# The last 64 rows of v copied in DRAM once per batch, one load of 96 rows per unit, and an order planned with longer issue times

## The chip, the cores and the metric

The kernel runs on one core of a Trainium2 chip. The metric is the device time of one execution in microseconds (us), the median of three runs. The engines are TensorE (PE, with its weight loads PEld), VectorE (DVE), ScalarE (ACT), GpSimd (POOL) and SyncE (SP); SP issues nearly all DMAs, into one hardware queue that 16 DMA engines serve. L12 is line 12 of the kernel before.

## The reference

An attention of two parts over 8 batches, 8 heads, 576 positions and 64 columns a head, then a feed-forward block over the 4,608 tokens. All numbers are fp32.

```python
q_d, k_d, v_d = (x.reshape(B, H, S // 4, 4, D).mean(axis=3) for x in (q, k, v))
out_up = np.repeat(sm_attn(q_d, k_d, v_d), 4, axis=2)      # attention of the means of four rows
mask = np.abs(pos[:, None] - pos[None, :]) < 4              # and a band of 7 positions
scores = np.where(mask, scale * q @ k.T, -1e9)
out_local = softmax(scores) @ v
x = (out_up + out_local).transpose(0, 2, 1, 3).reshape(4608, 512)
h = x @ w_in                                                # 512 x 2048
out = (h * np.clip(h + 3, 0, 6) / 6) @ w_out                # 2048 x 512
```

The change touches `v_d`, the sums of four rows of v. Of 144 such sums a head, 128 fill the 128 partitions, and 16 are left over: those of the last 64 rows of v.

## The kernel before

**Work.** Attention is cut into 32 units: a batch b and a pair of heads hp (four pairs). The feed-forward block is cut into nine chunks of 512 tokens; a chunk has 16 blocks f of 128 of the 2,048 columns. For each f, `gemm1` (L1053, matmuls at L1059) forms h, ACT and DVE apply the gate (L1065, L1069), `hi` and `lo` (L1071, L1075, both through L121, L119 or L1077) split it into a rounded part and a rest, and `gemm2` (L1104, L1109) adds its share of the output. An fp32 product is three matmuls of such parts. The last two chunks are computed together by sums and differences of blocks (L1141 on). A chunk needs the attention of its tokens, so attention and feed-forward work are interleaved.

**A unit.** q and k come in with four DMAs each (`ldt`, L373), and DVE turns them (`turn`, L379) and sums them by fours (`pool4`, L411 on DVE). v comes in by windows (`ldv`, L433), and for the sums of four rows by `ld4`: `ld4(0)` loads 128 rows of 2 KB, four rows of v each (L439), and `ld4(1)` the last 64 rows of v. In units of which the probabilities of both heads are multiplied together (26 of the 32) the 16 rows of 2 KB are wanted four times, on partitions 0, 16, 64 and 80, so `ld4(1)` is four DMAs of 16 rows (L444). `sum4` (L446) sums them by fours, multiplies with a mask by head and clears partitions 32 to 63 and 96 to 127. Units 0 to 5 ("alone") load the 64 rows with one DMA (L441). Probabilities go through DRAM to be turned: the downsampled ones by `pd` (`put_d` L612, `get_d` L620 and L625), the local ones by `pl` (`put` L639, `get` L647). The sum of both parts is written by `add` (L766 on DVE); the parts of x split from that are what `gemm1` reads.

**Bursts.** From unit 8 on PE's attention work stands in bursts (`plan_burst`, L329): the scores of a new unit (L523, L668, L718) and the products with v of the unit two before it (L761).

**Order.** The program is straight-line code, and a list scheduler writes its order: `Plan.emit` (L1798) has a cost for every operation (`COST`, and numbers at the call of `op`), due times from `T0`, `TC`, `TF` and `UNIT_T`, moved for each unit by `SHIFT`, and gives each engine the ready operation that is due first. Where an operation may run on several engines, `PEN` holds what an engine adds to its due time. DMAs are modelled by `Queue` (L1723): the time to issue one (`BEGUN`), to serve it (`PACKET`) and to land (`LAND`), and a ring of eight, since every DMA waits for the semaphore of the DMA eight before it. Each engine executes its list in order, so an instruction that waits holds all behind it on its engine. Dummy matmuls (L1449) stand in front of the first GEMM.

Of the kernel before, what the change touches and what calls it, by code (L numbers as in the profile page):

```python
# [8 lines left out]
F32 = mybir.dt.float32  # L9
# [8 lines left out]
B, H, S, D = 8, 8, 576, 64  # L18
DM, DFF = 512, 2048
P = 128  # L20
# [36 lines left out]
def tile_local_down_attention_moe(ctx, tc, q_all, k_all, v_all, _qk_loc, _v_loc, w_in, w_out, ident_d, _mask_d, out):  # L57
# [179 lines left out]
    def src(t, first, ap):  # L237
        return bass.AP(tensor=t.tensor, offset=t.offset + first * ROW, ap=ap)
# [117 lines left out]
    def plan_unit(b, d, u, row0, k0, kv, PS, masked, early_user, due):  # L356
# [62 lines left out]
        for kind, t in (("q", q_all), ("k", k_all)):  # L419
            hk = kind, un  # L420
            if b < BY_PE:
                a = turned[kind] = [evs["qk".index(kind)], evs[2]]
            else:
                l = op("SP", 2.0, partial(ldt, t, kind), loads if b == 1 else [], take=[("qk", hk)], size=dma(4 * S, 128), nd=4)
                a = turned[kind] = [op("DVE", 0.72, partial(turn, kind), [l], lag=BEHIND[0 if b == 1 else 1])]
            pooled[kind] = early_user(op(
                on("pool4", 1.0), 0, partial(pool4, kind), a, take=[("p4" + k0, hk)]))
# [8 lines left out]
        def ld4(g):  # L436
            st["raw", g] = raw = buf("raw" + k0, ("v", un, g), [P, 4, ROW])
            if g == 0:
                nc.sync.dma_start(raw, src(v_all, row0, [[4 * ROW, P], [1, 4 * ROW]]))  # L439
            elif alone:  # L440
                nc.sync.dma_start(raw[:4 * KR, 0], src(v_all, row0 + 4 * P, [[ROW, 4 * KR], [1, ROW]]))  # L441
            else:
                for first in (0, KR, D, D + KR):
                    nc.sync.dma_start(raw[first:first + KR], src(v_all, row0 + 4 * P, [[4 * ROW, KR], [1, 4 * ROW]]))  # L444

        def sum4(g, eng):  # L446
            if "vd" not in st:
# [35 lines left out]
        if direct:  # L483
            sums = [begun["vr"], op({"POOL": on("sum4", 1.0)["POOL"]}, 0, partial(sum4, 0), [begun["v", d]],
                                    take=[("vd" + k0, un)], free=[("raw4", (0, d))])]
        for g in range(0 if direct else 2):
            rk = "raw" + k0, ("v", un, g)
            l = op("SP", 0.5, partial(ld4, g), take=[rk], size=dma(P, 512) if alone and g else dma((P, 2 * NAR)[g], 2048), nd=1 if alone else 1 + 3 * g)
            if alone and g:
                bk = PS, ("v4", un, g)  # L490
                a = op("PE", 0.34, partial(sum_pe, g), [l], take=[bk], free=[rk], lag=LAGT, rec=2)
                sums.append(op(on("ev", ROW), 0, partial(evict_v, g), [a], take=[("vd" + k0, un)], free=[bk]))
            else:
                sums.append(op(on("sum4", 1 + g), 0, partial(sum4, g), [l], take=[("vd" + k0, un)], free=[rk], lag=BEHIND[3]))

# [546 lines left out]
    def plan_moe(n):  # L1042
# [6 lines left out]
        for f in range(NF):  # L1049
# [42 lines left out]
            last1 = a  # L1092
            gemms.append(a)
            b = op("ACT", 0.04 + size / 1130, relu, [a], take=[("t" + k0, ("t", key))])
            c = op("DVE", 0.07 + size / 960, gate, [b], free=[("h", key)])
            d = op(on("ghi", size), 0, hi, [c], take=[("gh" + k0, ("gh", key))], lock=True)
            st["ready"] = [d, op(on("gl", size), 0, lo, [d], take=[("gl" + k0, ("gl", key))], free=[("t" + k0, ("t", key))],
                                 lock=True)]
# [390 lines left out]
        plan.emit(warm, gemms[0], busy)  # L1489


T0, TC, TF, LAG = 60.12, 81.59, 5.26, 2.0
UNIT_T = (4.0, 20.34, 23.11, 24.0, 25.01, 24.0, 24.0, 21.51)
EARLY = 0.7
SLACK = (3.35, 24.0, 49.24, 41.62, 33.95, 31.63, 36.96, 13.02)
PRE, GATE = 4, 14

AHEAD = 2

FIRST = 6.8, 2.92  # L1500


HK = DM // 2
# [19 lines left out]

EARLY_Z = 14, 28

LAGT = 0.5

BEHIND = [-0.29, 0.65, 0.0, -0.16]

LAGW = 2.16  # L1530

# [1 line left out]
ORDERED = ("raw", "qk", "v", "vd", "P", "Pd", "Pl", "PT", "od", "p4", "st", "a", "o0", "o1", "o2", "o3", "z", "sx", "ue", "uo", "ghb", "glb")  # L1533
HOP, FREE = 0.1, 0.1

BOTH, KEEP = ("h0x", "h1x"), -7.57

MARGIN = 0.43

PAIR0 = 8  # L1540

SHIFT = [
# [4 lines left out]
]  # L1547

STAY = 8.33

IDLE, COLD = (0.22, 0.1, 0.75), 7.2

# [2 lines left out]
PACKET = {64: 38, 128: 11.5, 512: 27.5, 576: 27, 1024: 50, 2048: 88, 4096: 170}  # L1555
BEGUN = {64: 0.41, 128: 0.52, 512: 0.67, 576: 0.65, 1024: 0.36, 2048: 0.45, 4096: 0.47, (512, 640): 0.49, (2048, 36): 0.4, (128, 384): 0.49}
LAND = {64: 1.3, 128: 1.25, 512: 2.0, 576: 1.45, 1024: 1.2, 2048: 1.5, 4096: 1.65, (512, 640): 1.2}
FRESH, TURNED, LANDS, SHORT = (3.2, 18.0, (512, 2048), 1.6), (0.7, 25.0), (2.4, 6.0), 0.16
HOPS = {("ACT", "DVE"): 0.14, ("ACT", "PE"): 0.19, ("ACT", "POOL"): 0.16, ("DVE", "ACT"): 0.13, ("DVE", "PE"): 0.19, ("DVE", "POOL"): 0.2,
        ("PE", "ACT"): 0.2, ("PE", "DVE"): 0.2, ("POOL", "ACT"): 0.075, ("POOL", "DVE"): 0.075, ("POOL", "PE"): 0.1,  # L1560
# [17 lines left out]
    "pull": {"ACT": (0.22, 0.0), "DVE": (0.17, 0.0)},  # L1578
}
PEN = {  # L1580
    "lo": {"DVE": 2.22},
    "low": {"DVE": 8.81},
    "whi": {"DVE": 12.96},
    "ghi": {"DVE": -5.51},
    "pool4": {"POOL": 26.99},
    "ev": {"DVE": 5.81},
    "sum4": {"POOL": -4.99},
    "norm": {"DVE": 68.37},
    "normd": {"DVE": 46.75, "ACT": 23.63},
    "minus": {"DVE": -10.56},  # L1590
    "xhi": {"DVE": 31.2},
    "xlo": {"POOL": -27.96},
    "gl": {"POOL": 5.88},
    "ob": {"DVE": 12.47},
    "pull": {"DVE": 0.92},
}


# [119 lines left out]
def dma(packets, size):  # L1718

    return Load([(packets, size)])  # L1720


class Queue:  # L1723
# [7 lines left out]
    def begin(self, t, size, n):  # L1731
        k = n // len(size.parts)
        for packets, each in [(p / k, e) for p, e in size.parts for _ in range(k)]:
            t = max(t, self.slot()) + BEGUN.get((each, round(packets)), BEGUN[each])
            while self.queued and sum(p for at, p in self.queued if at > t) + packets / 16 > QUEUED:
                left = [at for at, _ in self.queued if at > t]
                if not left:
                    break
                t = min(left)
            self.queued = [x for x in self.queued if x[0] > t]  # L1740
            took = service(packets, each)
            if each in FRESH[2] and FRESH[0] < t < FRESH[1]:
                took *= FRESH[3]
            took = max(took, SHORT) + (TURNED[0] if t > TURNED[1] and self.big != (each == 4096) else 0.0)
            self.big = each == 4096
            self.flow = max(self.flow, t + (LANDS[0] if t < LANDS[1] else LAND[each, round(packets)] if (each, round(packets)) in LAND else LAND[each])) + took
            self.landed.append(self.flow)
            self.queued.append((self.flow, packets / 16))
        return t, self.flow


class Plan:
# [5 lines left out]
    def op(self, eng, cost, fn, after=(), take=(), free=(), size=0, dl=None, lag=0.0, lock=False, rec=0, nd=1, kind=None):  # L1758
        o = Op(len(self.ops), eng, cost, fn, take, size, dl)
        o.kind = kind  # L1760

        o.rec, o.nd = rec, nd
        o.lag, o.lock = lag, {True: ("DVE", "POOL"), False: ("POOL",)}[lock]
        self.ops.append(o)
        for a in after:
            self.dep(o, a)
        for r in free:
            self.free_after(r, [o])
        return o
# [308 lines left out]
```

## Time and profile before

| | us |
|---|---|
| median of three runs (899.37 to 902.68) | 900.11 |
| the profiled execution | 899.97 |
| its span | 898.2 |
| PE busy | 883.5 (98%) |
| DVE busy | 628.1 (70%) |
| ACT busy | 402.4 (45%) |
| POOL busy | 219.4 (24%) |

The granted TensorE clock is 1.00 over the whole span. The chain that ended last is PE for 90%, SP's queue for 3%, DMA for 3%. A chain of waits is followed back from the last instruction to what released it; where it lies on PE, PE has work, and where it leaves PE, something came late. The windows show in which stretch that is.

### The profile page before, as it was taken

The page shows a single profiled execution, that of the slowest core. Times are in us where ns is not written, and L with a number is a line of the kernel's source. Part 1 is how long each engine was busy: PE and PEld are TensorE (multiplying, and loading weights), DVE is VectorE, ACT ScalarE, POOL GpSimd, SP SyncE. Part 2 cuts the span into 40 slices and gives each one's busy share as a digit, 9 for nine tenths or more (in the row PEclk, how much of TensorE's full clock was granted, in tenths as well). Part 3 has the DMA queues.
Part 4 walks back from the last instruction along what each step waited for, and adds up shares of the span by engine and source line. Part 5 has one row for each costly group of instructions (what it writes and reads, how often), then busy time and mean ns, then how long its engine had stood idle before and what let it go on. Part 6 is the DMA issues. An engine that isn't in the chain of part 4 may idle for free.

```text
span 898.2 us, 19662 instructions
## 1 busy us (share of the span) xinstructions
PE 883.5 (98%) x7067; PEld 720.6 (80%) x7067; DVE 628.1 (70%) x1182; ACT 402.4 (45%) x1397; POOL 219.4 (24%) x292
## 2 busy tenths in 40 slices
PE   8999999999999999999999999999999999999998
PEld 6677878887887888888887888888778888888886
DVE  7998988766766467676767666567666899965430
ACT  6787644545474145444544426144443444331100
POOL 4554633232232011211111312103222125301000
PEclk9999999999999999999999999999999999999999
DMA  9999576556566356655367516857657002223011
GB/s 228 204 284 327 128 174 129 114 117 127 99 147 129 67 106 133 130 113 104 78 141 148 115 33 142 244 121 178 147 121 181 2 24 70 87 78 117 17 31 48
DMA packets 325985, 111.95 MB, mean 125 GB/s; under 512 B 258687, under 2 KB 306943, under 8 KB 325887
## 3 DMA queue, kind: packets, MB, share of 16 engines
q1 hardware_dynamic: 325206, 109.92, 52.1%
q8 instruction: 56, 0.92, 0.4%
q10 hardware_dynamic: 680, 0.77, 0.3%
q14 instruction: 43, 0.34, 0.1%
HBM read 79.58 MB, written 31.05 MB: 123 GB/s over the span
## 4 chain that ended last, share of the span: by engine, by line
PE 90%; SPq 3%; DMA 3%; DVE 2%; ACT 1%; issue 1%; ACTq 0%; DVEq 0%
PE o L1109 32%; PE h L1059 32%; PE o L1407 5%; PE o L1292 4%; PE a L1407 2%; PE h L1407 2%; PE a L1292 2%; PE h L1292 2%; PE a L718 2%; PE h L761 1%; PE a L523 1%; DMA arena<-in_k_dram 1%; DMA arena<-in_q_dram 1%; PE h L668 1%; PE a L506 1%
## 5 line engine op out<-in xcount | busy, mean ns | idle before, releaser
L1109 PE MATMUL o<-wp,rounded 128*128 128x512 f32 x1344 | 322.7, 392 | 0.0
L1059 PE MATMUL h<-rounded,wp 128*128 128x512 f32 x1344 | 315.5, 390 | 4.6 <-DVE arena L766 3.3
L1059 PEld LDWEIGHTS h<-rounded,wp 128*128 128x128 f32 x1344 | 251.3, 188 | 59.4 <-issue 6.3
L1109 PEld LDWEIGHTS o<-wp,rounded 128*128 128x128 f32 x1344 | 249.7, 188 | 53.4 <-issue 0.4
L1065 ACT ACTIVATE arena<-h 128x512 f32<-128x512 f32 x112 | 66.5, 594 | 114.8 <-PE h L1059 113.6
L1069 DVE SCALAR_TENSOR_TENSOR arena<-arena,h 128x512 f32<-128x512 f32 x112 | 76.0, 678 | 42.3 <-ACT arena L1065 41.8
L1077 DVE TENSOR_TENSOR rounded<-arena,rounded 128x512 fp32r<-128x512 f32 x80 | 58.0, 725 | 37.1 <-PE o L1109 35.5
L573 ACT ACTIVATE arena<-arena 128x64 f32<-128x64 f32 x240 | 80.1, 336 | 0.4
L1077 POOL TENSOR_TENSOR rounded<-arena,rounded 128x512 fp32r<-128x512 f32 x32 | 43.8, 1370 | 129.5 <-PE o L1109 72.7
L119 ACT CAST rounded<-arena 128x512 fp32r<-128x512 f32 (+6 forms) x61 | 38.8, 640 | 49.5 <-DVE arena L1069 24.3
L121 DVE CAST rounded<-arena 128x512 fp32r<-128x512 f32 (+2 forms) x89 | 40.3, 455 | 28.9 <-PE o L1109 10.5
L379 DVE STREAM_TRANSPOSE arena<-arena 128x576 f32<-128x576 f32 x56 | 43.0, 769 | 24.6 <-DMA arena<-in_k_dram 12.8
L454 POOL TENSOR_TENSOR arena<-arena 96x256 f32<-96x256 f32 (+1 forms) x32 | 24.2, 756 | 138.3 <-DMA arena<-in_v_dram 134.7
L693 ACT ACTIVATE arena<-h 128x144 f32<-128x144 f32 x24 | 7.0, 291 | 96.7 <-PE h L677 96.6
L573 ACT ACTIVATION_READ_ACCUMULATOR arena<-arena 128x1 f32 x240 | 45.2, 188 | 0.0
L1407 PE MATMUL o<-wp,rounded 128*128 128x512 f32 (+1 forms) x204 | 43.8, 376 | 0.0
L1407 PEld LDWEIGHTS o<-wp,rounded 128*128 128x128 f32 x204 | 36.8, 188 | 7.1
L411 DVE TENSOR_REDUCE arena<-arena 128x144 f32<-128x576 f32 x53 | 38.6, 739 | 2.8 <-PE h L523 2.7
L455 POOL TENSOR_TENSOR arena<-arena 96x128 f32<-96x128 f32 (+1 forms) x32 | 15.1, 471 | 81.8 <-PE h L677 80.3
L452 DVE TENSOR_REDUCE arena<-arena 128x128 f32<-128x512 f32 (+1 forms) x22 | 23.7, 1078 | 15.8 <-PE h L668 6.9
L635 DVE STREAM_TRANSPOSE arena<-arena 128x384 f32<-128x384 f32 (+1 forms) x52 | 23.4, 464 | 14.5 <-DMA arena<-pd 14.0
L654 DVE STREAM_TRANSPOSE arena<-arena 128x640 f32<-128x640 f32 x26 | 21.9, 841 | 14.8 <-DMA arena<-pl 14.4
(260 smaller groups left out, 1206.4 us busy)
## 6 DMA issues: line engine op xcount, KB each, us to landing
arena<-in_v_dram SPq DMA_DIRECT2D x58, 160.0 KB
pl<-arena SPq DMA_DIRECT2D x26, 320.0 KB
arena<-pl SPq DMA_DIRECT2D x104, 80.0 KB
rawp<-in_w_in_dram SPq DMA_DIRECT2D x16, 512.0 KB
rawp<-in_w_out_dram SPq DMA_DIRECT2D x16, 512.0 KB
arena<-in_q_dram SPq DMA_DIRECT2D x112, 72.0 KB
arena<-in_k_dram SPq DMA_DIRECT2D x112, 72.0 KB
arena<-in_v_dram SPq DMA_DIRECT2D x28, 256.0 KB
```

The lines of the kernel that those rows point to most:

```text
L119: nc.scalar.copy(out_, in_)
L121: eng.tensor_copy(out_, in_)
L379: nc.vector.transpose(out=qk[kind], in_=qk[kind])
L411: eng.tensor_reduce(out=t, in_=x.rearrange("e (q r) -> e q r", r=4), op=ALU.add, axis=AX.X)
L573: nc.scalar.activation(x[:, j], x[:, j], AF.Exp, bias=m[:, j:j + 1], scale=0.125, accum_out=s[:, j:j + 1])
L1059: nc.tensor.matmul(st["ps"], win[f][:, wt, kk * P:(kk + 1) * P], xs[part][:, kk], start=(kk == 0 and i == 0), stop=(kk == NK - 1 and i == ...
L1065: nc.scalar.activation(st["t"], st["ps"], AF.Relu, bias=3.0)
L1069: nc.vector.scalar_tensor_tensor(out=t, in0=t, scalar=6.0, in1=st["ps"], op0=ALU.min, op1=ALU.mult)
L1077: eng.tensor_tensor(st["gl"], st["t"], st["gh"].bitcast(F32), op=ALU.subtract)
L1109: nc.tensor.matmul(otile[n, m], gt[:, ms], wout[f][:, wt], start=(f == 0 and i == 0), stop=(f == NF - 1 and i == 2),)
L1292: nc.tensor.matmul(ps[which], stationary(w, wt, kb), xs[x, kb][:, part], start=first and kb == 0 and q == 0, stop=last and kb == 1 and q = ...
L1407: nc.tensor.matmul(otile[n, m][:, cs], gt[:, ms], wout[f][:, wt, cs], start=(f == order[0] and i == 0), stop=(f == order[-1] and i == 2 an ...
```

## The change

`ends` is new. Once for each batch from 1 to 7 it copies, from DRAM to DRAM, the last 64 rows of v of all four pairs of heads, six times each: 24 pieces of 32 KB. `ld4(1)` then is one DMA of 96 rows of 2 KB from that copy, in place of the four of 16 rows; the 96 rows are six times the 16, so partitions 0 to 31 and 64 to 95 hold what they held before. The copy of batch b is planned behind a mark, the k load of unit 3 for the copy that follows batch 1 and of unit 1 of the previous batch for the others (the first two have none), and the 96-row load depends on the copy of its batch. That is 78 DMA issues less and 7 more.

The planner's gate costs 0.07 us more (at c), its issue times are 1.06 times and its landings 0.25 us longer behind 130 us (`SLOWER`), and the tables are others: `T0`, `LAG`, `UNIT_T`, `SLACK`, `FIRST`, `LAGT`, `BEHIND`, `KEEP`, `MARGIN`, `SHIFT`, `STAY`, `PEN`. Lines after L425 stand 2 to 13 further down in the changed kernel: L433 is L435, L439 is L441, L444 is L446, L766 is L777, L1059 is L1070.

```diff
@@ plan_unit @@
+                if kind == "k" and hp == (3 if b == 1 else 1):
+                    begun["mark", b] = [l]
...
-                for first in (0, KR, D, D + KR):
-                    nc.sync.dma_start(raw[first:first + KR], src(v_all, row0 + 4 * P, [[4 * ROW, KR], [1, 4 * ROW]]))
+                t = begun["ends", b]
+                nc.sync.dma_start(
+                    raw[:D + 2 * KR], bass.AP(tensor=t.tensor, offset=t.offset + hp * 6 * KR * 4 * ROW, ap=[[4 * ROW, D + 2 * KR], [1, 4 * ROW]]))
+
+        def ends():
+            begun["ends", b] = t = dram.tile([NHP * 6 * KR, 4 * ROW], F32, name=f"ends{b}", tag=f"ends{b}")
+            nc.sync.dma_start(
+                bass.AP(tensor=t.tensor, offset=t.offset, ap=[[6 * KR * 4 * ROW, NHP], [KR * 4 * ROW, 6], [1, KR * 4 * ROW]]),
+                src(v_all, row0 - hp * S + 4 * P, [[S * ROW, NHP], [0, 6], [1, KR * 4 * ROW]]))
...
+        if not alone and ("end", b) not in begun:
+            begun["end", b] = [op("SP", 0.5, ends, begun.get(("mark", b - 1), []), size=dma(NHP * 6 * KR, 2048))]
         for g in range(0 if direct else 2):
-            l = op("SP", 0.5, partial(ld4, g), take=[rk], size=dma(P, 512) if alone and g else dma((P, 2 * NAR)[g], 2048), nd=1 if alone else 1 + 3 * g)
+            l = op("SP", 0.5, partial(ld4, g), begun["end", b] if g and not alone else [], take=[rk], size=dma(P, 512) if alone and g else dma((P, D + 2 * KR)[g], 2048), nd=1)
@@ plan_moe @@
-            c = op("DVE", 0.07 + size / 960, gate, [b], free=[("h", key)])
+            c = op("DVE", 0.14 + size / 960, gate, [b], free=[("h", key)])
@@ tables @@
-T0, TC, TF, LAG = 60.12, 81.59, 5.26, 2.0
+T0, TC, TF, LAG = 58.23, 81.59, 5.26, 2.03
...
-    26.07, 0.93, 45.62, 26.7, -0.45, 17.22, 31.26, 31.47,
+    -15.5, 18.9, 45.62, 36.78, 21.85, 21.74, 31.26, 31.47,
...
+SLOWER = 130.0, 1.06, 0.25
...
-    "ghi": {"DVE": -5.51},
+    "ghi": {"DVE": 50.88},
@@ Queue.begin @@
-            t = max(t, self.slot()) + BEGUN.get((each, round(packets)), BEGUN[each])
+            late = t > SLOWER[0]
+            t = max(t, self.slot()) + BEGUN.get((each, round(packets)), BEGUN[each]) * (SLOWER[1] if late else 1.0)
```

Three places in the order of the instructions. In the first, SP's queue some 18 issues from the start, L373 are the loads of q and k of the first unit of batch 1, L439 and L441 its rows of v. Before:

```order
L439 DMA arena_65<-in_v_dram 128x512
L441 DMA arena_65<-in_v_dram 64x128
L373 DMA arena_65<-in_q_dram 32x18x32 x4
L373 DMA arena_65<-in_k_dram 32x18x32 x4
L433 DMA arena_65<-in_v_dram 64x5x128
L175 DMA rawp0_555<-in_w_in_dram 128x1024
```

And the same place now, where `ends1` is the copy of batch 1:

```order
L441 DMA arena_65<-in_v_dram 128x512
L443 DMA arena_65<-in_v_dram 64x128
L451 DMA ends1_346<-in_v_dram 24x1x8192
L373 DMA arena_65<-in_q_dram 32x18x32 x4
L373 DMA arena_65<-in_k_dram 32x18x32 x4
L435 DMA arena_65<-in_v_dram 64x5x128
```

The copy stands in front of the unit's loads of q and k.

The second place is SP's queue around the last unit of batch 2 (`pl2_3` and `pd2_3` are its probabilities in DRAM). Before:

```order
L639 DMA pl2_3_2667<-arena_65 128x5x128
L439 DMA arena_65<-in_v_dram 128x512
L444 DMA arena_65<-in_v_dram 16x512 x4
L433 DMA arena_65<-in_v_dram 64x5x128
L647 DMA arena_65<-pl2_3_2667 32x20x32 x4
L620 DMA arena_65<-pd2_3_2641 32x12x32 x4
L625 DMA arena_65<-pd2_3_2641 24x3x16 x4
```

Now, with the copy of batch 4:

```order
L650 DMA pl2_3_2657<-arena_65 128x5x128
L441 DMA arena_65<-in_v_dram 128x512
L446 DMA arena_65<-ends2_1351 96x512
L451 DMA ends4_2664<-in_v_dram 24x1x8192
L435 DMA arena_65<-in_v_dram 64x5x128
L658 DMA arena_65<-pl2_3_2657 32x20x32 x4
L631 DMA arena_65<-pd2_3_2640 32x12x32 x4
L636 DMA arena_65<-pd2_3_2640 24x3x16 x4
```

Four loads of 16 rows are one of 96 rows, and a copy stands behind it, ahead of the twelve reads of `pl` and `pd`.

The third place is DVE's list in the stretch that turns the first q and k of batch 1 (L379) and sums them by fours (L411); `first` is the x of the first chunk. Before:

```order
L379 STREAM_TRANSPOSE arena_65<-arena_65 128x576
L766 TENSOR_TENSOR first_478<-o3_522,early_228 128x288
L766 TENSOR_TENSOR first_478<-o1_523,early_228 128x224
L411 TENSOR_REDUCE arena_65<-arena_65 128x144
L379 STREAM_TRANSPOSE arena_65<-arena_65 128x576
L766 TENSOR_TENSOR first_478<-a1_447,arena_65 128x64
L766 TENSOR_TENSOR first_478<-o1_523,early_228 128x64
L411 TENSOR_REDUCE arena_65<-arena_65 128x144
L766 TENSOR_TENSOR first_478<-o0_593,early_228 128x288
```

And now:

```order
L777 TENSOR_TENSOR first_481<-a1_450,arena_65 128x64
L121 COPY early_505<-a0_512 16x3x2x48
L594 RECIPROCAL early_229<-early_229 128x10
L121 CAST rounded_66<-first_481 128x288
L121 COPY arena_65<-a1_525 16x128
L777 TENSOR_TENSOR first_481<-o3_528,early_229 128x288
L777 TENSOR_TENSOR first_481<-o1_529,early_229 128x224
L379 STREAM_TRANSPOSE arena_65<-arena_65 128x576
L777 TENSOR_TENSOR first_481<-o1_529,early_229 128x64
L121 COPY early_229<-a0_564 128x144
L411 TENSOR_REDUCE arena_65<-arena_65 128x144
L379 STREAM_TRANSPOSE arena_65<-arena_65 128x576
```

Sums of `first`, a cast and copies have moved ahead of the first turn.

## Rows read from the trace of the kernel before

**Rows 1.** The page's head and its part 1: busy us, share, instructions.

```profile
span 898.2 us, 19662 instructions
PE 883.5 (98%) x7067; PEld 720.6 (80%) x7067; DVE 628.1 (70%) x1182; ACT 402.4 (45%) x1397; POOL 219.4 (24%) x292
```

**Rows 2.** Windows: us, busy of PE, PEld, DVE, ACT, POOL, clock, DMA share, GB/s.

```profile
20.00:40.00 20.00, 18.67 (x321) 12.57 (x320) 18.58 (x51) 16.90 (x57) 11.52 (x15) 1.00 0.92 188
40.00:60.00 20.00, 19.01 (x174) 14.16 (x173) 19.47 (x37) 17.09 (x35) 9.94 (x8) 1.00 0.96 284
200.00:220.00 20.00, 18.79 (x185) 15.32 (x184) 13.96 (x30) 9.92 (x49) 6.91 (x12) 1.00 0.71 136
260.00:280.00 20.00, 19.76 (x187) 16.07 (x187) 11.25 (x24) 10.60 (x48) 7.47 (x10) 1.00 0.72 146
280.00:300.00 20.00, 18.89 (x83) 15.69 (x84) 15.78 (x33) 9.29 (x40) 2.49 (x3) 1.00 0.71 146
460.00:480.00 20.00, 18.04 (x182) 14.71 (x181) 13.25 (x28) 8.15 (x38) 3.69 (x5) 1.00 0.65 134
660.00:680.00 20.00, 18.95 (x185) 15.62 (x184) 13.84 (x30) 8.79 (x39) 4.86 (x8) 1.00 0.67 175
880.00:898.20 18.20, 13.79 (x73) 11.72 (x71) 1.12 (x2) 1.58 (x3) 0.00 (x0) 1.00 0.20 58
```

**Rows 3.** Chain of waits, 449 to 480 us: start, us, what.

```profile
459.53 1.90 DMA arena<-in_v_dram
...
469.52 0.44 SPq L373
470.00 3.75 DMA arena<-in_q_dram
...
475.38 0.45 DVE arena L766
```

**Rows 4.** Chain of waits, 272 to 284 us.

```profile
276.56 3.15 DMA arena<-in_q_dram
```

**Rows 5.** Chain of waits, 660 to 681 us.

```profile
666.21 1.07 SPq L444
...
671.13 1.55 DMA arena<-pd
```

**Rows 6.** SP's timeline, 500 to 503 us: start, us, instruction.

```profile
500.38 0.45 SPq L439 DMA_DIRECT2D arena<-in_v_dram  x1
500.93 1.76 SPq L444 DMA_DIRECT2D arena<-in_v_dram  x4
```

**Rows 7.** The page's DMA queues: packets, MB, share of 16 engines.

```profile
q1 hardware_dynamic: 325206, 109.92, 52.1%
...
q10 hardware_dynamic: 680, 0.77, 0.3%
```

**Rows 8.** Windows of 2 us, without engines: us, clock, DMA share, GB/s.

```profile
16.00:18.00 2.00, 1.00 1.10 240
...
24.00:26.00 2.00, 1.00 0.73 101
26.00:28.00 2.00, 1.00 0.78 123
28.00:30.00 2.00, 1.00 0.72 123
48.00:50.00 2.00, 1.00 1.04 416
```

**Rows 9.** Chain of waits, 0 to 62 us.

```profile
26.03 3.97 DMA arena<-in_k_dram
30.13 0.78 DVE arena L379
...
39.87 1.38 PE h L1059 x6
```

**Rows 10.** Chain of waits of the whole span, at 90 us.

```profile
90.01 5.44 PE h L1059 x24
```

More of the change, by code (lines that the diff above doesn't have):

```diff
@@ L1489, in tile_local_down_attention_moe @@
         plan.emit(warm, gemms[0], busy)
-T0, TC, TF, LAG = 60.12, 81.59, 5.26, 2.0
-UNIT_T = (4.0, 20.34, 23.11, 24.0, 25.01, 24.0, 24.0, 21.51)
+T0, TC, TF, LAG = 58.23, 81.59, 5.26, 2.03
+UNIT_T = (4.0, 20.34, 23.11, 26.04, 24.95, 25.46, 25.23, 21.75)
 EARLY = 0.7
-SLACK = (3.35, 24.0, 49.24, 41.62, 33.95, 31.63, 36.96, 13.02)
+SLACK = (3.35, 24.0, 54.31, 33.27, 33.21, 32.06, 36.96, 12.27)
 PRE, GATE = 4, 14
 AHEAD = 2
-FIRST = 6.8, 2.92
+FIRST = 6.8, 2.79
 HK = DM // 2
@@ L1524 @@
 EARLY_Z = 14, 28
-LAGT = 0.5
-BEHIND = [-0.29, 0.65, 0.0, -0.16]
+LAGT = 0.54
+BEHIND = [-0.29, 0.67, 0.0, -1.22]
 LAGW = 2.16
@@ L1534 @@
 HOP, FREE = 0.1, 0.1
-BOTH, KEEP = ("h0x", "h1x"), -7.57
-MARGIN = 0.43
+BOTH, KEEP = ("h0x", "h1x"), -13.5
+MARGIN = 0.39
 PAIR0 = 8
 SHIFT = [
[4 rows of a table removed]
[4 rows of a table added]
 ]
-STAY = 8.33
+STAY = 7.12
 IDLE, COLD = (0.22, 0.1, 0.75), 7.2
@@ L1580 @@
 PEN = {
-    "lo": {"DVE": 2.22},
+    "lo": {"DVE": 51.66},
     "low": {"DVE": 8.81},
     "whi": {"DVE": 12.96},
-    "ghi": {"DVE": -5.51},
+    "ghi": {"DVE": 50.88},
     "pool4": {"POOL": 26.99},
[L1586 to L1595, printed above, removed]
+    "ev": {"DVE": 16.72},
+    "sum4": {"POOL": -8.29},
+    "norm": {"DVE": 67.25},
+    "normd": {"DVE": 26.95, "ACT": 16.43},
+    "minus": {"DVE": -29.45},
+    "xhi": {"DVE": 11.05},
+    "xlo": {"POOL": -95.23},
+    "gl": {"POOL": 1.62},
+    "ob": {"DVE": 12.78},
+    "pull": {"DVE": -5.73},
 }
@@ L1745, in begin @@
             self.big = each == 4096
-            self.flow = max(self.flow, t + (LANDS[0] if t < LANDS[1] else LAND[each, round(packets)] if (each, round(packets)) in LAND else LAND[each])) + took
+            self.flow = max(self.flow, t + (SLOWER[2] if late else 0.0) + (LANDS[0] if t < LANDS[1] else LAND[each, round(packets)] if (each, round(packets)) in LAND else LAND[each])) + took
             self.landed.append(self.flow)
```

6 rows, old and new, of the table SHIFT are left out of this document.

## The prediction

> **What bounds the kernel now.** I read the page's busy shares first, then a table of 20 us windows, then the chain of waits around each hole in TensorE, then SyncE's (SP's) own timeline. PE is busy for 883.5 of 898.2 us [rows 1], so 14.7 us are all that a better order can win. The windows say where these lie: 1.33 + 0.99 between 20 and 60 us, 1.21 at 200, 0.24 + 1.11 around 280, 1.96 at 460, 1.05 at 660, 4.41 at the end [rows 2]; the rest stands in the first 20 us, before the inputs are in. The windows not shown have PE busy throughout. So from 60 us on PE is the bound, anything that makes PE later there adds to the end, and the middle holds 5.6 us in four holes.
>
> The chain names what closes each hole. At 474 us a load of v lands, then a q load that SP issued last at 469.52 takes 3.75 us, DVE turns it and only then adds the sum (L766) that PE waits for [rows 3]. At 280 us a q load of 3.15 us stands ahead of the same sum [rows 4]. At 671 us the last read of `pd` (1.55 us) ends the wait; ahead of it SP had spent 1.07 us and more on the small loads of L444 [rows 5]. In all three the data arrives late because SP issued late. (In the hole at 200 us PE waits for the same kind of sum.) Each hole follows two bursts of attention work that the order of before puts closer than 16 us of PE work.
>
> **The change, part by part.** The sum is made against the profiled execution, 899.97 us (its span and 1.77 us around it); the median of the runs is 900.11, 0.14 above it.
>
> *Loads removed.* A unit's four loads at L444 hold SP for 1.76 us, one load of 128 rows of the same 2 KB pieces for 0.45 us [rows 6]. One 96-row load instead of four of 16 is nearest to the latter, so SP gains about 1.3 us in each of 26 units, 34 us of SP time. PE gains only where SP is the late link: the holes at 280, 460 and 660 us. The longer issue times in the planner and the new SHIFT table pull the same way: the new order spaces the bursts around 200 us evenly, at 22.8 us of PE work where it was 15.3 and 33.7, though elsewhere five close pairs remain of six. Nothing makes sure that a hole closes rather than moves. Bounds: 0 to -5.6 us; I take -4, three of the four.
>
> *The copy, in DRAM.* Each is 24 pieces of 32 KB, 786,432 bytes. How many of the 16 DMA engines carry it decides its price, and no transfer of before has this form: its source counts 4 (then 6 with stride zero), its target 24. What the trace has is a packet count. The two hardware queues moved 325,206 + 680 = 325,886 packets [rows 7]. The shapes of all 1,049 transfers give 310,208 pieces of data, which leaves 15,678: one more packet for each engine that took part. At 16 engines each it would be 16,784. It comes out at exactly 15,678 if a transfer uses the largest number of engines up to 16 that divides its row count: the 104 reads of 24 rows on 12, the 94 stores of 36 rows on 12, the eight stores of 4 rows on 4, and so on (8 of 8, 10 of 20, 14 of 28). A copy that reads in 4 blocks and writes in 24 then has 4 engines, if both sides must divide, or 12, if only the target counts. The rate of one engine: 416 GB/s at a share of 1.04 is 25 bytes per ns, 240 at 1.10 is 13.6 [rows 8]. So 4 engines need 7.9 us (196,608 bytes each) to 14.4 us, 12 engines 2.6, 16 engines 2.0. I take 4 engines at 7.9 us and keep 2.0 and 14.4.
>
> The Trainium skill ("DMA: Bandwidth & Descriptors", section on why a DMA increments its semaphore by 16) has k as the largest number up to 16 that divides the slowest dimensions of both access patterns, and its "Rules for kernel authors" say that a leading zero-stride broadcast of few copies confines a DMA to as many engines. It speaks against this change; by it the copy has 4 engines, and 16 if it were wrong. By that rule the count of 15,678 agrees for one-sided row counts; no run of before shows the two-sided case.
>
> *The first copy.* In the new order it stands in front of the q and k loads of the first unit of batch 1. Before, the last piece of that k takes 3.97 us from 26.03, DVE turns it in 0.78, and the chain goes on from there to the first GEMM at 39.87 [rows 9]. On the four engines that the copy holds, k's share waits for 7.9 us, less what these engines have idle between 24 and 30 us: shares of 0.73, 0.78 and 0.72 in three windows of 2 us leave 1.5 us [rows 8]. So k lands some 6.3 us later. The new DVE order has about five small rows (2 us) moved ahead of that turn, so that much of the delay is filled with work that had stood behind it: +4. Bounds: +0.5 (16 engines), +10 (11 to 14 us of copy and the same filling). Nothing gives it back, since PE has under 1 us idle in 40 to 60 us and none after.
>
> *The second copy* is issued among the weights' loads; by the order 27 us of PE work lie between it and its first reader: 0. If the weights' loads are delayed by it, the loss is at most its 7.9 us, and I have no sign of that.
>
> *Copies 3 to 7.* From batch 3's copy on, each stands just ahead of the unit's reads of `pl` and `pd`, which the next burst needs. On the four engines a read waits for the whole copy: 0.5 us of issue, 7.9 of copy, about 2 for the reads and v loads that queue on the same engines, 1.55 of landing [rows 5], 12 us in all. SP's own reach matters too: in the order of semaphores each DMA waits for the one eight before it, so seven more go and the eighth waits for the copy. In the order stand 11.4, 11.4, 14.1 and 14.1 us of PE work (at 0.227 us for a matmul of 512 columns, [rows 10]) between copies 4, 5, 6 and 7 and the bursts, and 8.7 for copy 3, with fewer reads behind it. I take 0.6 + 0.6 + 0 + 0 + 0.8 = +2. Bounds: 0 (12 or 16 engines), +13 (11 us of copy: 15.5 needed, 4.1 + 4.1 + 1.4 + 1.4 + 2), +23 at 14.4.
>
> *The rest.* Four more dummy matmuls stand before the first GEMM (0.9 us at 0.227), in time in which PE waits for k anyway: 0, or +0.9 if it doesn't. The 96 rows move 196 KB as four times 16 rows moved 131 KB, 65 KB more per unit or 0.16 us of 16 engines; hidden under a DMA share of 0.65 to 0.72 [rows 2]. The wait of the 96-row load for the copy of its batch: copies go one batch ahead, 60 us and more, so nothing waits, the first batch apart, whose reader stands 30 us behind. Moving `lo` and `ghi` off DVE (their penalties rise to 51) loads ACT and POOL; at 45% and 24% [rows 1] they have room: 0.
>
> Sum: 899.97 - 4 + 4 + 2 = 902.0.
>
> **The rivals.**
> *Copies on 12 or 16 engines* (0.25). For it: the target's 24 rows divide by 12. Against it: the source has only 4 blocks. Copies cost 0.5 at the start and nothing later, the holes close: 899.97 - 4 + 0.5 = 896, between 894 and 899.
> *Slow copies* (0.18), the other side by a distance. Engines that share with other queues' work run nearer to the 13.6 than to the 25 bytes per ns. It decides from the point at which a copy lands later than 9.5 us after its issue. At 11.4 us: 899.97 - 4 + 8 + 13 = 917; at 14.4 us and no hole closed up to 933. Against it: from 80 us on the shares are 0.65 to 0.72, so the engines aren't full.
> *The holes aren't SP's* (0.15). DVE works in order, and in two holes its sum stands behind a transpose that waits for a load; an order that puts it there again keeps the hole however fast SP issues. For it: the sum itself (L766) needs nothing from that load. The middle stays at 5.6, start +4, copies +2: 906.
>
> **How the numbers follow.** The likeliest (0.42) is 902, itself 898 to 906. What a measurement of this kernel can tell from no change is 0.5%, 4.5 us: under 895.6 is faster, over 904.6 slower. Faster / same / slower: the likeliest 0.02 / 0.29 / 0.11, wide copies 0.13 / 0.12 / 0, slow copies 0 / 0.02 / 0.16, holes kept 0 / 0.05 / 0.10; together 0.15 / 0.48 / 0.37. The range 894.5 to 915 leaves out the best of the wide copies and the upper half of the slow ones.
>
> **What would show it.** The count of packets: the seven copies add 28 small ones at 4 engines, 84 at 12, 112 at 16. The first k load of batch 1: landing at 36 us (4 engines), 30 (16). The windows: 40 to 60 us with PE as full as before but 4 us behind in its work; the holes at 280, 460 and 660 gone or moved; SP's waits naming the copies. SP's issue of the 96-row load: about 0.45 us. I am wrong if the copies land in 3 us, if the first GEMM starts no later than before, or if new holes of over 2 us stand behind copies 6 and 7.

## The result and the profile after

The changed kernel takes 910.48 us (median of six runs, 908.66 to 911.33) against 899.74 for the kernel before on the same chip: a ratio of 1.0104 with a 95% interval of 1.0083 to 1.0126. It is slower, by the forecast's own line of 904.6 too, an outcome to which the forecast gave 0.37. The time lies inside the range of 894.5 to 915, but 8.5 us above the likeliest case of 902. The profiled execution has a span of 908.5 us, 10.3 more than before.

The first lines of the page that answer to [rows 1] and [rows 7], of the changed kernel:

```profile
span 908.5 us, 19584 instructions
...
PE 889.8 (98%) x7071; PEld 723.8 (80%) x7071; DVE 625.2 (69%) x1168; ACT 423.0 (47%) x1424; POOL 211.1 (23%) x283
...
q1 hardware_dynamic: 324986, 117.12, 53.3%
...
q10 hardware_dynamic: 680, 0.77, 0.3%
```

PE is busy 6.3 us longer for four matmuls more, and idle for 18.7 us where it was 14.7. Busy time that grows without work points to a slower clock. The granted clock in the windows says where (the columns are those of [rows 2]):

```profile
20.00:40.00 20.00, 17.40 (x265) 11.78 (x264) 14.86 (x43) 12.01 (x40) 11.55 (x16) 0.84 0.75 171
40.00:60.00 20.00, 19.65 (x213) 13.32 (x212) 18.74 (x35) 16.89 (x44) 8.87 (x8) 0.99 1.04 315
60.00:80.00 20.00, 17.89 (x124) 13.67 (x124) 17.19 (x31) 13.95 (x20) 11.87 (x10) 0.91 0.91 273
120.00:140.00 20.00, 18.84 (x127) 14.79 (x126) 16.97 (x29) 9.31 (x24) 8.96 (x6) 1.00 0.53 151
180.00:200.00 20.00, 17.09 (x178) 13.83 (x176) 10.41 (x21) 7.80 (x38) 3.70 (x7) 1.00 0.54 135
200.00:220.00 20.00, 19.65 (x181) 16.12 (x182) 15.99 (x35) 10.24 (x52) 4.94 (x9) 0.91 0.73 144
260.00:280.00 20.00, 20.00 (x192) 16.59 (x191) 10.82 (x22) 10.14 (x40) 3.25 (x3) 1.00 0.63 150
280.00:300.00 20.00, 20.00 (x122) 16.42 (x124) 13.43 (x28) 10.13 (x41) 3.99 (x6) 1.00 0.59 117
460.00:480.00 20.00, 20.00 (x192) 16.58 (x191) 14.15 (x31) 6.87 (x28) 4.26 (x8) 1.00 0.67 146
660.00:680.00 20.00, 19.87 (x190) 16.18 (x189) 13.94 (x28) 8.79 (x41) 7.10 (x11) 1.00 0.78 183
```

The four holes of before are all but gone: 280 and 460 have PE full, 660 lacks 0.13 us, and the 0.35 that 200 lacks is the end of a new hole. New ones stand in the first 80 us (8.11 us idle in all against 4.60), at 128 us (1.16) and from 197.1 to 200.35 us (3.26), and three stretches, about 34 to 41, 68 to 71 and 201 to 204 us, run at the lower level of TensorE's clock, 1.2 GHz. The first of them in windows of 2 us (us, PE busy, clock, DMA share, GB/s):

```profile
24.00:26.00 2.00, 2.00 (x57) 1.00 0.29 95
26.00:28.00 2.00, 1.68 (x32) 1.00 0.27 115
30.00:32.00 2.00, 1.52 (x46) 1.00 0.33 50
32.00:34.00 2.00, 0.38 (x2) 0.89 0.81 128
34.00:36.00 2.00, 2.00 (x13) 0.50 0.74 177
36.00:38.00 2.00, 2.00 (x47) 0.50 0.98 330
```

At 24 to 28 us the DMA share is 0.27 to 0.29 in a stretch in which before had 0.73 to 0.78 [rows 8]: worked out from the share, a little over 4 of 16 engines are busy. The packet records show the first copy's 24 pieces of 32 KB from 22.2 to 30.7 us. DVE then waits for q, and PE for a sum that stands behind that wait on DVE (timelines of DVE and of PE; the bracket is the idle time before and its releaser):

```profile
32.59 0.78 DVE L379 STREAM_TRANSPOSE arena<-arena 128x576 f32<-128x576 f32 x1 [3.31 <-DMA arena<-in_q_dram]
...
34.74 0.78 DVE L379 STREAM_TRANSPOSE arena<-arena 128x576 f32<-128x576 f32 x1 [0.39 <-DMA arena<-in_k_dram]
```

```profile
33.62 0.87 PE L754 MATMUL o<-ident,early 128*128 128x128 f32 x3 [2.10 <-DVE first L777]
...
45.12 1.17 PE L1070 MATMUL h<-rounded,wp 128*128 128x512 f32 x4
```

PE stands still for 2.10 us, and then the clock is at half. L1070 at 45.12 us is the first GEMM; in the same view of the kernel before it starts at 39.63 us (39.87 in the chain of [rows 9]).

The hole at 197 us is in the waits of PE (in total, times, longest), in the chain of waits and in SP's timeline:

```profile
PE h L1070 <- DVE arena L1080: 4.8, 4, 3.3
```

```profile
184.45 10.55 DMA pl<-arena
...
196.53 2.23 DMA arena<-pl
...
198.88 0.85 DVE arena L665
199.73 0.58 DVE arena L1080
```

```profile
182.87 0.70 SPq L451 DMA_DIRECT2D ends<-in_v_dram  x1
184.45 0.38 SPq L650 DMA_DIRECT2D pl<-arena  x1
187.76 0.67 SPq L435 DMA_DIRECT2D arena<-in_v_dram  x1
195.06 1.97 SPq L658 DMA_DIRECT2D arena<-pl  x4
```

Copy 3 is issued at 182.87 us, by the packet records its last piece ends at 193.71, and the write of `pl` behind it lands only at 195.0. SP can't issue the reads of `pl` before, and everything behind those in SP's list waits too. The last read lands at 198.76 us; DVE turns it (L665) and only then computes the gate (L1080) that PE waits for. As at the start, PE stands for a piece of DVE's work that needs nothing from the late load and stands behind it in DVE's list.

### The profile page after: what moved, and what is told of

Its sections match the earlier page's. It is cut to its first block, busy times and chain, and to the rows that moved or that the text cites. A ratio compares the mean times of both kernels' runs of the same rounds, so it can differ in the third digit from the quotient of the medians.

```text
span 908.5 us, 19584 instructions
## 1 busy us (share of the span) xinstructions
PE 889.8 (98%) x7071; PEld 723.8 (80%) x7071; DVE 625.2 (69%) x1168; ACT 423.0 (47%) x1424; POOL 211.1 (23%) x283
## 4 chain that ended last, share of the span: by engine, by line
PE 78%; SPq 5%; DMA 4%; DVE 3%; ACT 2%; issue 1%; POOL 0%; ACTq 0%; DVEq 0%; POOLq 0%
PE o L1120 29%; PE h L1070 26%; PE o L1418 4%; PE o L1303 4%; PE a L1418 2%; PE h L1418 2%; PE a L1303 2%; SPq L658 2%; PE h L1303 2%; PE a L729 1%; PE h L772 1%; DMA arena<-pl 1%; DMA pl<-arena 1%; SPq L373 1%; PE a L534 1%
## 5 line engine op out<-in xcount | busy, mean ns | idle before, releaser
L1070 PE MATMUL h<-rounded,wp 128*128 128x512 f32 x1344 | 318.7, 392 | 5.0 <-DVE arena L1080 4.8
L1070 PEld LDWEIGHTS h<-rounded,wp 128*128 128x128 f32 x1344 | 252.3, 189 | 60.6 <-DVE arena L1080 7.0
L1080 DVE SCALAR_TENSOR_TENSOR arena<-arena,h 128x512 f32<-128x512 f32 x112 | 76.0, 679 | 55.6 <-ACT arena L1076 55.4
L119 ACT CAST rounded<-arena 128x512 fp32r<-128x512 f32 (+4 forms) x92 | 57.8, 632 | 93.8 <-DVE arena L1080 29.0
L1088 POOL TENSOR_TENSOR rounded<-arena,rounded 128x512 fp32r<-128x512 f32 x28 | 38.6, 1382 | 101.6 <-PE o L1120 43.5
L379 DVE STREAM_TRANSPOSE arena<-arena 128x576 f32<-128x576 f32 x56 | 42.9, 769 | 13.5 <-DMA arena<-in_q_dram 8.1
L560 ACT ACTIVATE arena<-arena 128x1 f32<-128x1 f32 (+1 forms) x78 | 15.0, 193 | 57.0 <-DVE arena L573 57.0
L665 DVE STREAM_TRANSPOSE arena<-arena 128x640 f32<-128x640 f32 x26 | 21.9, 841 | 25.1 <-DMA arena<-pl 25.0
L601 POOL TENSOR_TENSOR arena<-arena 128x640 f32<-128x640 f32 (+1 forms) x18 | 21.2, 1178 | 76.0 <-DVE arena L594 40.0
L411 DVE TENSOR_REDUCE arena<-arena 128x144 f32<-128x576 f32 x49 | 36.1, 742 | 2.4 <-PE h L534 2.1
L461 DVE TENSOR_REDUCE arena<-arena 128x128 f32<-128x512 f32 (+1 forms) x24 | 25.7, 1075 | 16.1 <-PE h L679 8.6
L211 POOL TENSOR_TENSOR wp<-early,wp 128x1024 fp32r<-128x1024 f32 (+1 forms) x11 | 25.5, 2321 | 24.5 <-ACT wp L119 23.7
```

Of the source, the lines that this page charges most:

```text
L119: nc.scalar.copy(out_, in_)
L379: nc.vector.transpose(out=qk[kind], in_=qk[kind])
L411: eng.tensor_reduce(out=t, in_=x.rearrange("e (q r) -> e q r", r=4), op=ALU.add, axis=AX.X)
L461: eng.tensor_reduce(out=vd, in_=raw.rearrange("p r e -> p e r"), op=ALU.add, axis=AX.X)
L1070: nc.tensor.matmul(st["ps"], win[f][:, wt, kk * P:(kk + 1) * P], xs[part][:, kk], start=(kk == 0 and i == 0), stop=(kk == NK - 1 and i == ...
L1080: nc.vector.scalar_tensor_tensor(out=t, in0=t, scalar=6.0, in1=st["ps"], op0=ALU.min, op1=ALU.mult)
```

## The experiments

Each is compared with the kernel before on the same chip; the ratio's 95% interval stands in brackets. Since the kernel before itself takes 899.7 to 901.5 us on these chips, runs are set against each other by their ratios. Theory A puts the loss down to the copies on four engines, theory B to the new order. Where an order is kept, the instructions of PE, DVE, ACT and POOL stand in the same sequence.

**No copies (e1).** The load reads v, with a step of zero for the six repeats:

```diff
-            nc.sync.dma_start(<ends: copy of 24 x 32 KB>)
-                    raw[:D + 2 * KR], <96 rows of ends>
+                    raw[:D + 2 * KR], src(v_all, row0 + 4 * P, [[0, 6], [4 * ROW, KR], [1, 4 * ROW]]))
```

> The changed kernel's order on every engine, but without the seven copies: each 96-row load reads v itself, six times the same 16 rows. Theory A (the seven copies on four engines make the kernel late, through a q load at the start and a write of pl behind copy 4, and the low clock that follows the two waits): all of the loss goes and the old holes stay closed, 895 to 899 us. Theory B (the retuned order puts waiting work in front of other work by itself, the copies add little): 906 to 911 us. In between, both.

Measured: 900.4 us, 0.9981 (0.9957 to 1.0005). The order is the same, the copies are gone and most of the loss with them; theory B's 906 falls. By the ratios e1 is 1.2% faster than the changed kernel; on the scale of 899.74 it stands at 898.0, inside theory A's 895 to 899. It is still 0.4% slower than e5 below, which has this order without copies and the four loads of before, a difference just clear of the noise: something costs here too. The load has changed as well, and with its six repeats it is itself narrow: e1's 324,530 + 680 packets are those of before less the 104 loads of 16 rows (32 packets each), plus 26 loads of 96 + 6. So each ran on six engines.

**Copies on six engines (e2).**

```diff
-  ap=[[6 * KR * 4 * ROW, NHP], [KR * 4 * ROW, 6], [1, KR * 4 * ROW]]),  src(..., [[S * ROW, NHP], [0, 6], [1, KR * 4 * ROW]])
+  ap=[[KR * 4 * ROW, 6], [6 * KR * 4 * ROW, NHP], [1, KR * 4 * ROW]]),  src(..., [[0, 6], [S * ROW, NHP], [1, KR * 4 * ROW]])
```

> The changed kernel with the copy's dimensions exchanged, the six repeats outermost, so that 6 divides both sides: 6 engines, 131,072 bytes each. If the number of engines follows the outermost counts of both sides: 42 end packets for the seven copies in place of 28, a copy in 5.3 to 6 us in place of 7.4 to 9.3. Theory A: the waits for the first q and for the write of pl shrink by some 2.5 us, so that the clock falls less, 900 to 905 us. Theory B: 909 to 911 us.

Measured: 902.13 us, 1.0001 (0.9981 to 1.0021). Two engines more a copy, and 1% of the kernel's time comes back. By the packet records a copy takes 5.6 to 7.8 us (7.4 to 9.3 in the changed kernel). How many engines took part is read from the packet count, with one end packet for each. The queue in e2:

```profile
q1 hardware_dynamic: 325000, 117.13, 54.0%
```

That is 14 more than in the changed kernel, two for each copy. In the changed kernel, 325,666 packets in all are those of before (325,886) less 3,328 for the four loads, plus 26 x (96 + 16) for the new load on 16 engines, plus 196: seven copies of 24 pieces and 4 end packets. So 4 engines there, 6 here.

**Copies on 16 engines (e3).** Four copies in place of one, 16 rows of 2 KB outermost on both sides:

```diff
+            for x in range(NHP):
+                nc.sync.dma_start(
+                    bass.AP(tensor=t.tensor, offset=t.offset + x * 6 * KR * 4 * ROW, ap=[[4 * ROW, KR], [KR * 4 * ROW, 6], [1, 4 * ROW]]),
+                    src(v_all, row0 + (x - hp) * S + 4 * P, [[4 * ROW, KR], [0, 6], [1, 4 * ROW]]))
```

> The changed kernel with each copy as four copies, one for each pair of heads, that read and write 16 rows of 2 KB outermost, so that 16 engines share each. The bytes are the same. 16 engines need about 2 us for the bytes of one old copy, SP three more issues of 0.4 to 0.7 us. Theory A (narrow copies): 896 to 901 us. Rival A2 (the bytes of the copies themselves in a full stretch, not how many engines carry them): the start stays late, 904 to 908 us. Theory B: 909 to 912 us.

Measured: 897.18 us, 0.9955 (0.9939 to 0.9970): faster than before, with the same bytes and 21 DMA issues more than the changed kernel. A2 (the bytes) falls with B: what the copies cost is their four engines. The pieces are smaller here too, 2 KB for 32 KB; but e2 kept the 32 KB, and its six engines alone had given back 1% of the 1.5%. Stretches of e3 (us, PE busy, clock, DMA share, GB/s, as in those of e5 and e7 below):

```profile
0.00:80.00 80.00, 74.02 (x871) 0.98 0.97 264
80.00:180.00 100.00, 100.00 (x722) 1.00 0.69 164
180.00:300.00 120.00, 120.00 (x1142) 1.00 0.64 134
```

**The start and the rest (e7, e8).** Copy 1 alone wide, and copies 2 to 7 alone:

```diff
+            if b == 1:      # e7;  e8: if b > 1
+                <the four wide copies of e3>
+            else:
                 <the copy of the changed kernel>
```

> The changed kernel with only the first copy, the one ahead of the first q and k loads of batch 1, on 16 engines (as four copies); copies 2 to 7 stay on four. The trace of the changed kernel puts 8.3 us of wait and low clock into the first 80 us, of which e3 keeps about 3. Theory A by places: the start gains some 5 us, the wait behind copy 4 stays: 903 to 906 us. If the start matters little: 908 to 911.

> The other half of e7: copy 1 stays on four engines, copies 2 to 7 are on 16. Theory A by places: the wait of 2.9 us behind copy 4 and its 1.2 us of low clock go, and small ones with them, some 5 to 7 us, while the start stays late: 903 to 906 us. If only the start matters: 908 to 911.

Measured: e7 908.51 us, 1.0079 (1.0055 to 1.0104); e8 902.0 us, 1.0006 (0.9988 to 1.0024). Theory A by places missed in both, in opposite directions: e7 came out where the start was to matter little, e8 slightly faster than forecast. Against e3, by the ratios, the narrow copy 1 costs 0.51% or 4.6 us (e8), and the narrow copies 2 to 7 cost 1.24% or 11.2 us (e7). Against the changed kernel, where the other copies are narrow, copy 1 is worth 0.25% or 2.2 us (e7, not clear of the noise) and copies 2 to 7 0.98% or 8.8 us (e8). The late start of the changed kernel probably hides part of the wait behind copy 2 (1.16 us idle there, 3.77 in e7), which no run tests. The wait that my expectations name after copy 4 is that of copy 3; I had miscounted. e7's stretches:

```profile
0.00:80.00 80.00, 73.48 (x870) 0.98 0.95 263
80.00:180.00 100.00, 96.23 (x697) 0.98 0.64 151
180.00:300.00 120.00, 115.96 (x1048) 0.99 0.61 135
...
420.00:560.00 140.00, 138.62 (x1119) 1.00 0.53 114
```

PE loses 3.77 us to waits and some 2 to the clock behind copy 2, 4.04 and some 1.2 behind copy 3, and 1.38 behind 6 and 7. SP stood for 12.91 us in the four reads of `pl` behind copy 2, with the weights' loads behind them; with the wide copies of e3 the same four take 6.11 us. SP's timeline of e7, in which L664 are those reads:

```profile
98.71 12.91 SPq L664 DMA_DIRECT2D arena<-pl  x4
```

**Copies 2 and 3 behind the writes and reads (e9).**

```diff
-            <the copy>
+            begun["late", b] = copy      # b = 2, 3
 ...
+            begun.pop(("late", 2))()     # behind get's four reads;  copy 3: behind get_d's eight
```

> The changed kernel, all copies on four engines, but copy 2 is issued behind the four reads of pl that stood behind it, and copy 3 behind the write and the reads of pl and pd of its unit, not in front. (Copy 3, issued at 182.9 us, is the one whose wait the earlier expectations put down to copy 4.) Theory by place (what counts is which transfer stands behind the copy): the hole of 1.2 us at 128 us, and 3.3 us with 1.2 us of low clock at 197, go, copy 1 still costs the start: 903 to 906 us. Rival (four busy engines cost as much wherever the copy stands): 908 to 911.

Measured: 911.49 us, 1.0116 (1.0079 to 1.0153). No gain: the other places cost as much. Copy 3 (L452 in e9) moved to 195.69 us, and now the windows of v behind it are late (chain of waits, e9):

```profile
195.69 0.70 SPq L452
196.38 0.04 issue
196.43 10.39 DMA arena<-in_v_dram
```

PE waited 3.8 us for that load. Behind this copy stood another transfer that the burst needs, and it landed 1.2 us after the copy's last piece (205.58 us by the packet records). That every place in this list would cost as much is not shown; one other was tried for each of the two copies.

**The clock (e10).** Eight dummy matmuls in front of the transposes that PE waits for behind copy 1:

```diff
+            if getattr(o.fn, "func", o.fn).__name__ == "trans":
+                if trans == 6:
+                    busy(8)
+                trans += 1
```

> The changed kernel with eight dummy matmuls in front of the transposes (L754) that TensorE waits for at 31.5 to 33.6 us behind the first copy: 1.8 us of dummy work inside a wait of 2.1. It tells the two parts of the start's loss apart. If the clock falls because TensorE stands still there: it stays at its upper level from 33.6 to 40.4, which gives back up to 3.4 us: 906 to 908 us. If the clock falls for another reason, or the late q load sets the pace of that stretch anyway: 909.5 to 911.5.

Measured: 912.42 us, 1.0130 (1.0092 to 1.0168); no gain. Windows of e10, the first 80 us and then some of 2 us at two standstills (us, PE busy, clock, DMA share, GB/s):

```profile
0.00:80.00 80.00, 72.28 (x843) 0.94 0.89 249
...
34.00:36.00 2.00, 2.00 (x18) 1.00 0.93 173
36.00:38.00 2.00, 1.58 (x44) 0.56 0.92 338
...
66.00:68.00 2.00, 0.83 (x9) 0.74 0.95 316
68.00:70.00 2.00, 2.00 (x5) 0.50 0.98 266
70.00:72.00 2.00, 2.00 (x6) 0.50 1.03 414
```

The clock is still up at 34 to 36 us, but PE then stands again, the clock falls at 36, and once more and for longer behind 66. The mean of the first 80 us is the same 0.94. Worked out from the windows, the first low stretch lasts some 3.4 us in e10 where it lasted 6.8, and yet the first GEMM starts at 44.88 us for 45.12. So in that stretch, where the work stands behind late loads, the low clock costs little of its own. For the later stretches the run shows nothing: the one behind 66 us became longer. That the first fall came later with the dummies agrees with its following the standstill; the run doesn't show more.

**The holes of before: SP's issues, or the order?** Four runs. One load for four in the order of before (e4, the six repeats read from v):

```diff
-                for first in (0, KR, D, D + KR):
-                    nc.sync.dma_start(raw[first:first + KR], src(v_all, row0 + 4 * P, [[4 * ROW, KR], [1, 4 * ROW]]))
+                nc.sync.dma_start(raw[:D + 2 * KR], src(v_all, row0 + 4 * P, [[0, 6], [4 * ROW, KR], [1, 4 * ROW]]))
```

> The kernel before in its own order, with one 96-row load (six times the same 16 rows, from v) in place of the four loads of 16 rows in each of 26 units. Step tested: SP's issue time is what closes late in the holes at 280, 460 and 660 us. If so, SP gains 1.3 us a unit and these holes shrink to under 1 us together: 896 to 897.5 us. Rival (DVE's place in the order keeps the holes): 899 to 900.5 us.

Measured: 905.17 us, 1.0040 (1.0022 to 1.0058): slower, and outside both expectations. One load on six engines is worse than four on 16: its issue takes 0.81 us, and the four reads of `pl` behind it 3.57 us of SP where they took 2.07 before. What the issues save, SP loses again in the reads behind, and more.

The same with the wide copies of e3 (e6; the load on 16 engines, the copies issued at `ld4(0)` of unit 1 of the batch before, batch 1 with its four loads):

```diff
+                if hp == 1 and b < B - 1:
+                    ends(b + 1, row0 + S * (NHP - 1))
```

> The kernel before in its own order, with the 96-row load on 16 engines (0.44 us of SP in e3, against 1.8 to 2.8 for the four) and the wide copies of e3, issued with the first rows of v of unit 1 of the batch before; batch 1 keeps its four loads. Step tested: SP's issue time is what is late in the holes. If so the three holes shrink: 896 to 898.5 us, ratio to before about 0.996. Rival (the place of the waits in the order keeps the holes, SP's time only moves): 899 to 903 us, ratio 0.999 to 1.003.

Measured: 907.33 us, 1.0066 (1.0042 to 1.0089), outside both expectations too. I had put four more issues (2.54 us in one place) into SP's fullest stretch, so it says little about the step. In e6 PE stands still for 2.83 us before 482.7 us, where the kernel before has no standstill.

The load on 16 engines without any copy (e12). It reads other rows of v, so it leaves out the right sums of the last 64 rows:

```diff
+                nc.sync.dma_start(raw[:D + 2 * KR], src(v_all, row0, [[4 * ROW, D + 2 * KR], [1, 4 * ROW]]))
```

> The kernel before in its own order, with one 96-row load on 16 engines in place of the four, and no copy: it loads 96 other rows of v (of the unit's first rows), so that the sums of the last rows are left wrong; bytes, engines and issue are those of the changed kernel's load. It is e6 without the copies. Step tested: SP's issue time closes late in the holes of before. If so: 896 to 898.5 us, ratio 0.995 to 0.998. Rival (the order keeps the holes; SP's saved time is spent in waits for the ring of eight): 899 to 902 us, ratio 0.998 to 1.002.

Measured: 896.43 us, 0.9952 (0.9930 to 0.9974), as the step said. SP in the stretch before the hole at 474 us, e12:

```profile
457.04 0.37 SPq L443 DMA_DIRECT2D arena<-in_v_dram  x1
457.46 2.60 SPq L646 DMA_DIRECT2D arena<-pl  x4
...
466.38 2.22 SPq L373 DMA_DIRECT2D arena<-in_q_dram  x4
```

The load takes 0.37 us for 1.76, the q load is issued some 2 us earlier than in the kernel before, and the holes at 474 and 672 us are closed; those at 200 and 280 remain (2.49 us idle in 180 to 300, against 2.61). In the profiled executions PE is idle for 2.94 us between 80 and 700 us where it was 5.70; that is 2.8 of the 4.3 us gained, and the rest, within the interval of some 2 us, isn't traced to a place.

And the new order with the four loads of before, without copies (e5):

```diff
-                    <one load of 96 rows>
+                for first in (0, KR, D, D + KR):
+                    nc.sync.dma_start(raw[first:first + KR], src(v_all, row0 + 4 * P, [[4 * ROW, KR], [1, 4 * ROW]]))
```

> The changed kernel's order on every engine, but the loads of before: four of 16 rows from v in each of 26 units, no copy. With e3 and e6 this separates the order from the loads. If the new order closes the holes of itself: 896 to 899 us, as e3. If the loads (SP's issue time, 1.3 us a unit) close them: holes of 3 to 6 us in the middle again, 901 to 905 us.

Measured: 895.57 us, 0.9941 (0.9918 to 0.9964), the lowest ratio of all, though not clear of e12 and e3, and faster than both kernels. Its stretches:

```profile
0.00:80.00 80.00, 74.44 (x901) 1.00 0.94 256
80.00:180.00 100.00, 100.00 (x797) 1.00 0.65 148
180.00:300.00 120.00, 119.40 (x1069) 1.00 0.60 121
...
560.00:700.00 140.00, 139.54 (x1225) 1.00 0.64 160
```

Behind the first 80 us PE is idle for 1.06 us to 700 us; before it was 5.70. So the order closes the holes by itself, with all of SP's issues still there. Order and issues each close holes, partly the same ones (474 and 672 us). That they don't add is likely but not shown: with both, e3 stands at 0.9955, no better than either alone, but it has the wide copies besides. The new order with the load on 16 engines and no copies was not run.

**The new costs, planned for four loads (e11).**

```diff
-            begun["end", b] = [op("SP", 0.5, ends, ...)]
-            l = op("SP", 0.5, partial(ld4, g), begun["end", b] if g and not alone else [], ..., nd=1)
+            l = op("SP", 0.5, partial(ld4, g), ..., nd=1 if alone else 1 + 3 * g)
```

> All the new tables, the gate's cost and the longer issue times, with the four loads of before and without the copies, and planned as such (e5 kept the order that was planned for copies). If the gain of e5 is that of the new costs in general: 894 to 897 us. If e5's order is one good order by chance among neighbours: 897 to 905.

Measured: 901.24 us, 0.9997 (0.9980 to 1.0015). With the same tables and costs, planned for what it issues, the order has 4.70 us of idle PE in 80 to 180 us. So e5's gain is that of one order, and not shown to be that of the new costs: its expectation for an order that is good by chance, 897 to 905 us, is the one that held.

## Why the prediction was right or wrong

*Engines of a copy: right.* Four, by the end packets (28 for seven copies); six where both outermost counts are 6. What was open, whether both sides count, is settled by the two. The Trainium skill's rule ("DMA: Bandwidth & Descriptors", the section on why a DMA increments its semaphore by 16) agrees with both counts. The duration was 7.4 to 9.3 us from first to last piece where 7.9 was forecast. But the first piece starts 1.5 to 4.4 us behind the start of the issue, for which the sum had 0.5, so the last piece ends 10.5 to 11.9 us behind it and not 8.4 (SP's timeline and packet records of the changed kernel).

*The holes of before, -4: right in size.* e12 gains 4.3 us (0.48% of 900) by one issue for four, as the step said, and e5 5.3 by the order alone; in the changed kernel the holes closed as well. What I had not seen is that the order can close them without SP's issues. The rival that the holes aren't SP's falls with e12 for two of them, at 474 and 672 us. The one at 280 I had counted as SP's too: it stayed in e12, as did that at 200, and both are closed by the order (0.60 us left in e5).

*The first copy, +4: right in size.* The first GEMM starts at 45.12 us for 39.63, 5.5 later (40.59 in e3), and e8 against e3 puts the copy's price at 4.6 us; with the other copies narrow it is 2.2, not clear of the noise. DVE turns k at 34.74 us for 30.13, 4.6 later where I had 6.3. The way was another one: q, not k, was late first, and a sum that PE needed stood behind DVE's wait.

*The second copy at nothing, and copies 3 to 7 at +2: wrong. This is the step that failed.* e7 against e3 makes them 11.2 us, the changed kernel against e8 8.8. Two terms were mis-sized. For copy 3 I set 0.8 us, by reads that wait for a copy. My own 12 us, less 8.7 us of PE work, would have made 3.3; "with fewer reads behind it" took the rest off without a row. PE then stood for 3.26 us, but both numbers behind the 3.3 were wrong, so the likeness is luck: the write that these reads read stood behind the copy as well, two transfers came one after the other, and from the issue of the copy to the last read's landing, 182.87 to 198.76, it was 15.9 us; and from that issue PE had 14.2 us of work up to its standstill at 197.1. For copy 2 I looked at its own reader, 27 us behind. The weights' loads behind it I had named, at up to 7.9 us, and put at nothing for want of a sign; the reads of `pl` behind it I hadn't. With the ring of eight SP stood in those for 11.97 us in the changed kernel and 12.91 in e7, and the weights' loads with it. Copies 4 to 7 came out near the 1.2 us forecast in sum, behind others than thought (0.23 us of idle behind copy 4 in the changed kernel, 1.43 behind 6 and 7). The parts don't quite add to the whole: by the ratios 0.9955 + 0.0051 + 0.0124 would be 1.0130, the changed kernel has 1.0104; in it PE, late from the start, waits 1.16 us behind copy 2 where e7 waits 3.77.

*The clock: not in the sum.* PE is busy 6.3 us longer in the profiled execution, 0.9 of it the four dummies by my own figure. The sum had nothing for this and gave no reason. At the start it costs little by itself (e10). What the stretches behind 66 and 201 us cost, no run separates from the waits ahead of them.

*The slow copies* were the rival nearest to the time (917). Its condition came true, and its reason didn't: every copy ended later than the 9.5 us behind its issue at which it was to decide, but one engine moved 23 to 27 bytes per ns, as the likeliest case took, and not 13.6. Most of the delay stands ahead of the first piece. That 910.48 lies inside the range is therefore partly luck: the likeliest case ended at 906, and what reaches on to 915 had been kept for engines of half the rate.

## What to carry to other kernels

Before a copy replaces small loads, work out its engines from the outermost counts of both sides, and give it 16; the same bytes then cost little here (e3) and on four engines 1.5% of the kernel. Price a long narrow transfer by everything behind it in the issuing queue, a write and the read of that write in series, and not by its own reader; and count its time from the issue, not from the first piece. And separate an order from the loads it was planned for: here the order alone was worth 0.6%, and the copies took away more than twice that.

## What the runs showed that was not expected

A load of 96 rows on six engines costs SP 0.8 us to issue, on 16 engines 0.44 (median of 26 in the changed kernel), and the four reads behind it in e4 took SP longer: it was slower than four loads of 16 rows (e4 against before, 1.0040). A standstill of PE of 2.1 us at 31.5 us was followed by half the clock for about 7 us, one of 1.16 us at 66 us by some 3 us of it, but one of 1.96 us at 474 us in the kernel before by none (the granted clock is 1.00 in that window of [rows 2]); no run here explains the difference. With copy 1 on the queue, a q load's four issues took SP 7.17 us where they had taken 4.83.
